# An attention and mixer kernel on one core: last tile of w_theta loaded and decoded earlier, epsilon added on VectorE, one q product moved behind the first theta product

## The chip, the cores and the metric

One core of one Trainium2 chip. The time is device microseconds (us) of one execution of the whole program; of the kernel before there are three timed runs, 1085.14, 1086.68 and 1089.25, and their median, 1086.68, is what the changed kernel's median is compared with. A further execution was taken with the hardware profiler; it took 1086.08 us.

## What is computed

The reference is a chain of three parts over 8 batches of 576 tokens and 512 channels (8 heads of 64). Attention without softmax comes first, then a mixer whose token weights turn with an angle theta, then a second mixer. What the change touches is attention and the start of the first mixer:

```python
kv = np.einsum('bhsd,bhse->bhde', k, v)
out = np.einsum('bhsd,bhde->bhse', q, kv)
rms = np.sqrt(np.mean(out * out, axis=-1, keepdims=True) + 1e-06)
x = out / rms * g_norm                      # then (b, s, h*d)
theta = x @ w_theta
zr, zi = x * np.cos(theta), x * np.sin(theta)
y = np.einsum('ts,bsd->btd', w_tok_r, zr) + np.einsum('ts,bsd->btd', w_tok_i, zi)
u = x + y
x = u + np.maximum(u @ w_ch, 0.0)
```

The inputs q, k, v are 32-bit floats; the weights (w_theta, w_tok, w_ch and so on) come as 64-bit floats and are turned into 32-bit ones on the chip.

## The kernel before

A batch's 576 tokens are worked in five tiles: four of 128 tokens (0 to 3) and one of 64 (4). Most products are made of three 16-bit products (a high and a low half of each operand, helper `mm3`, lines 101 to 107). In batch 0 alone, q products, turns and theta products are 32-bit ones, which take several passes over the array. The work around the change is all in batch 0, at the start of the program, and goes through these steps:

- **Loads.** SP's queue asks for everything in the order in which the program is written: w_theta's four tiles (`theta_weight`, `load` at line 148), k and v of batch 0 (L382, L386, L392), the first 128 tokens of q (L406), the rest of q (`load_q`, L421), then the token weights `wmr` (L233).
- **Decoding** (`decode`, lines 161 to 174) of a 64-bit weight tile: one ScalarE pass (L164) and three VectorE passes (L172, L173, L174) in which 32-bit words are shifted and joined. w_theta goes into `wt`; the token weights into `wm0v`, `wm1v` and so on, and from there into high and low halves `wmh` (L245, ScalarE) and `wml` (L247, VectorE).
- **kv** (L438), the product of k and v, ends in `kvbd`.
- **attend** (lines 450 to 506), written `a0` to `a4` in the schedule: the q product `po` (L458), its square on ScalarE (L471), the sum over a head's 64 channels on VectorE (`ss`, L473), on GpSimd the addition of epsilon (L474) and the power of -0.5 (`ri`, L475), the scaled `x` on VectorE (L478), and in batch 0 a turn of `x` on TensorE (`px`, L488) that ScalarE copies out (`xt`, L490).
- **rotate** (lines 551 to 593), written `r0` to `r4`: the theta product `pt` (L563; for tile 4 it is L604), then in turns ScalarE and VectorE: rounding (L574, L578), sine, absolute value, cosine (L581 to L583), the product of both with `x` (L586), the 16-bit halves `zh` (L590) and `zl` (L593).
- **outer** (`X0` to `X4`): the token mix, 16-bit products `pa` and `pb` of `zh`, `zl` with `wmh`, `wml` (lines 105 to 107).

Each of these is a generator, and one line of text sets the order in which they are started (line 1027); every start also lets all open ones go one step further (`go` and `advance`, lines 985 to 997). `w` in it starts the next token weight. What the engines get in the end is settled by a list scheduler, which moves instructions within each engine's list except those that are held in the written order (`tc.keep_in_program_order`, here by `held` for batch 0, lines 425 to 427). Each engine then works off its list strictly in order.

Of the kernel before, what the change touches and what calls it, by code (L numbers as in the profile page):

```python
# [14 lines left out]
ALU = mybir.AluOpType  # L15
# [13 lines left out]
def attn_mixer_kernel(  # L29
# [4 lines left out]
    nc = tc.nc  # L34
# [3 lines left out]
    KD = DM // P  # L38
# [25 lines left out]
    def bank(name):  # L64
        return ps.tile([P, 512], F32, tag="ps", name=name)
# [58 lines left out]
    eps = const.tile([P, H], F32, name="eps")  # L124
# [9 lines left out]
    wt = const.tile([P, KD, DM], F32, name="wt")  # L134
# [11 lines left out]
    def load(dst, src):  # L146

        tc.keep_in_program_order(nc.sync.dma_start(dst, src))

    wp = []  # L150
# [3 lines left out]
    def gated(ins, behind):  # L154

        tc.add_manual_dep(
            ins.ins, (turned_xt[0] if behind is turned_xt else turned_zh[behind]).name,
            mybir.DependencyInfo(mybir.DependencyClass.NoSync, mybir.DependencyReason.DATA), reason="behind",
        )

    def decode(val, raw, behind=None):

        bits = val.bitcast(I32)
        first = nc.scalar.activation(val, raw[..., 1].bitcast(F32), AF.Copy, scale=2.0**-112)  # L164
        if behind is not None:
            gated(first, behind)
        if wp:

            tc.keep_in_program_order(first)
        yield  # L170
        place = placed if wp else lambda ins: ins
        place(nc.vector.tensor_scalar(bits, bits, 3, None, ALU.logical_shift_left))  # L172
        place(nc.vector.scalar_tensor_tensor(bits, raw[..., 0], 29, bits, ALU.logical_shift_right, ALU.bitwise_or))  # L173
        place(nc.vector.scalar_tensor_tensor(bits, raw[..., 1], -(2**31), bits, ALU.bitwise_and, ALU.bitwise_or))  # L174
# [23 lines left out]
    def theta_weight(j):  # L198

        if w_theta.dtype == F32:  # L200
            load(wt[:, j], w_theta[j * P:(j + 1) * P])
            yield
        else:
            raw = stg.tile([P, S, 2], I32, tag="raw", name=f"wt{j}r")[:, :DM]
            load(raw.rearrange("p n w -> p (n w)"), w_theta.bitcast(I32)[j * P:(j + 1) * P])
            yield
            yield from decode(wt[:, j], raw)

    def theta_split(j):

# [186 lines left out]
    def load_heads(b, whole=True):  # L397
        o = Batch()
        o.b, o.zh = b, None
        o.kv = []  # L400
        for r in range(NR + 1 if b < 2 else 3):
            load_kv(o, r)
        o.q = fp.tile([P, HP, SM + P], F32, tag="q", name=f"q{b}", bufs=1)
        qs = qT[b].rearrange("h p s -> p h s")
        if b == 0:
            nc.sync.dma_start(o.q[:, :, :P], qs[:, :, :P])  # L406
        elif whole:
            load_q(o, 0)
        return o

    def load_q(o, at):
        qs = qT[o.b].rearrange("h p s -> p h s")
        if o.b + 1 < B:

            part = qs[:, :, at:]
            (ps_, _), (hs, _), (ss_, _) = part.ap
            parts = [(o.q[:, :, at:], bass.AP(part.tensor, part.offset, [[ps_, P], [hs, HP], [ss_, SM + P - at]]))]
        else:
            parts = [(o.q[:, :, at:S], qs[:, :, at:]), (o.q[:, :, S:], qs[:, :, SM:])]
        for dst, src in parts:  # L420
            ins = nc.sync.dma_start(dst, src)  # L421
            if o.b in (2, 3):
                tc.keep_in_program_order(ins)

    def held(o, ins):
        if o.b == 0:
            tc.keep_in_program_order(ins)
# [22 lines left out]
    def attend(o, r):  # L450

        b = o.b
        if r == 0:
            o.R = mp.tile([P, KD, S], F32, tag="R", name=f"R{b}", bufs=2)
            o.x, o.xt = {}, {}
        po = bank(f"po{b}{r}")
        for hp in range(HP):
            held(o, nc.tensor.matmul(po[:, hp * P:(hp + 1) * P], o.q[:, hp, r * P:(r + 1) * P], kvbd[:, hp, :], start=True, stop=True))  # L458
        po3 = po.rearrange("p (h d) -> p h d", d=D)
        ss = fp.tile([P, H], F32, tag="ss", name=f"ss{b}{r}", bufs=3)  # L460
        ri = fp.tile([P, H], F32, tag="ri", name=f"ri{b}{r}", bufs=3)
        xs = fp.tile([P, 2, DM], F16, tag="xs", name=f"xs{b}{r}", bufs=2) if b else None
        x = o.x[r] = fp.tile([P, DM], F32, tag="x", name=f"x{b}{r}", bufs=NR + 1)
        xt = o.xt[r] = fp.tile([P, 2, KD, P], F16, tag="xt", name=f"xt{b}{r}", bufs=NR + 1)
        if b == 0:
            xt = o.xt[r] = xt.rearrange("p a k t -> p (a k t)").bitcast(F32).rearrange("p (k t) -> p k t", k=KD)

        x3 = x.rearrange("p (h d) -> p h d", d=D)
        place = beside(o)
        yield  # L470
        place(nc.scalar.activation(x3, po3, AF.Square, scale=D**-0.5))  # L471
        yield
        held(o, place(nc.vector.tensor_reduce(ss, x3, axis=AX.X, op=ALU.add)))  # L473
        nc.gpsimd.tensor_tensor(ss, ss, eps, ALU.add)  # L474
        nc.gpsimd.tensor_tensor(ri, ss, mhalf, ALU.pow)  # L475
        yield
        yield
        held(o, place(nc.vector.tensor_tensor(x3, po3, ri.unsqueeze(2).to_broadcast([P, H, D]), ALU.mult)))  # L478
        n = SR if r == NR else P
        R, by = o.R[:, :, r * P:r * P + n], SW if r == NR else gs  # L480
        if r == NR and b == 2:
            R = x[:, :KD * SR].rearrange("p (k t) -> p k t", k=KD)
        if b == 0:

            yield
            px = bank(f"px{r}").rearrange("p (k t) -> p k t", k=KD)
            for kk in range(KD):
                held(o, nc.tensor.transpose(px[:, kk, :], x[:, kk * P:(kk + 1) * P], ident))  # L488
            yield
            turned_xt.append(nc.scalar.activation(xt, px, AF.Copy, scale=gt).ins)  # L490
            if r == NR:
                nc.scalar.activation(R, px[:, :, :n], AF.Copy, scale=by)
            return
        if b > 1:
            yield
        place(nc.scalar.activation(xs[:, 0, :], x, AF.Copy))
        yield
        place(nc.vector.tensor_tensor(xs[:, 1, :], x, xs[:, 0, :], ALU.subtract))
        place(nc.sync.dma_start_transpose(xt.rearrange("p a k t -> p (a k) t"), xs.rearrange("p a d -> p (a d)")))
        if 0 < b < 3 and r < NR:  # L500
            return
        for _ in range(3 if b > 1 else 2):
            yield
        place(nc.scalar.activation(R, xt[:, 0, :, :n], AF.Copy, scale=by))
        yield
        place(nc.vector.scalar_tensor_tensor(R, xt[:, 1, :, :n], by, R, ALU.mult, ALU.add))
# [13 lines left out]
    def beside(o):  # L520
        return placed if o.b > 1 else lambda ins: ins

    def channel_weights():

        if w_ch.dtype == F32:
            return [weight_tile(stg, w_ch, wc, j, DM, SW, "wc") for j in range(KD)]
        raws = []
        for j in range(KD - 1):
            raw = stg.tile([P, S, 2], I32, tag="raw", name=f"wc{j}r")[:, :DM]
            nc.sync.dma_start(raw.rearrange("p n w -> p (n w)"), w_ch.bitcast(I32)[j * P:(j + 1) * P])  # L530
            raws.append(raw)
        return [weight_tile(stg, w_ch, wc, j, DM, SW, "wc", raw=raw, behind=g) for j, (raw, g) in enumerate(zip(raws + [None], (NR, NR + 1, NR + 1, NR + 2)))]
# [452 lines left out]
    def go(unit, lead=False):  # L985
        advance()
        next(unit)
        (leading if lead else pending).append(unit)
# [16 lines left out]
    def spare(n=1):  # L1005
        for _ in range(min(n, len(extra))):
            go(extra.pop(0))
# [6 lines left out]
    for j in range(KD):  # L1014
        if j == 2:
            o = load_heads(0)
        go(theta_weight(j))
        if j == max(2, 1):
            load_q(o, P)
    for part in range(2):  # L1020
        go(kv(o, part))
# [2 lines left out]
    extra += mix_weights()  # L1024
    nxt = load_heads(1)
    later = channel_weights()
    for what in "a0 . . a1 a4 a2 a3 r0 w r1 r4 w r2 r3 X0 X1 k w w w X4 A0 X2 A1 s0 s1 s2 s3 X3 A4 A2 A3 U".split():
        if what == ".":
            advance()
        elif what == "w":  # L1030
            spare()
        elif what == "k":
            for part in range(2):
                go(kv(nxt, part))
        elif what == "U":
            go(mixed(o))
        else:
            unit = {"a": attend, "r": rotate, "X": outer, "s": residual}[what[0].replace("A", "a")]
            go(unit(nxt if what[0] == "A" else o, int(what[1])))
# [42 lines left out]
    for b in range(B):  # L1082
# [71 lines left out]
        o, nxt = nxt, after  # L1154
# [52 lines left out]
```

## Time and profile before

| | us |
|---|---|
| median of three runs | 1086.68 |
| the profiled execution | 1086.08 |
| its span | 1084.3 |
| TensorE busy (98% of the span) | 1064.3 |
| VectorE busy (74%) | 806.8 |
| ScalarE busy (52%) | 565.0 |
| GpSimd busy (17%) | 186.6 |

The span runs from the first to the last instruction of the profiled execution. Times of rows count from its start. In what follows the engines have the profile's names: PE is TensorE, DVE VectorE, ACT ScalarE, POOL GpSimd, SP the engine that asks for most transfers.

### The profile page before, as it was taken

How to read it: one execution, taken by the hardware profiler on the slowest of the kernel's cores; microseconds unless marked ns; L12 is line 12 of the kernel's file. 1: busy time of each engine (PE TensorE's matmuls, PEld its weight loads, DVE VectorE, ACT ScalarE, POOL GpSimd, SP SyncE). 2: the span in 40 equal slices, each digit the busy share in tenths (PEclk: the TensorE clock that was granted, in tenths of full speed). 3: DMA queues.
4: the chain of work that ended last, by engine and by line, in shares of the span. 5: the costliest groups of instructions: out<-in, count | busy, mean ns of one | idle time of the engine just before them, and what ended most of it. 6: DMA issues, size and time to landing. Idle time of an engine off the chain costs nothing.

```text
span 1084.3 us, 21468 instructions
## 1 busy us (share of the span) xinstructions
PE 1064.3 (98%) x8857; PEld 812.4 (75%) x8857; DVE 806.8 (74%) x1431; ACT 565.0 (52%) x950; POOL 186.6 (17%) x256
## 2 busy tenths in 40 slices
PE   6999998999999999999999999999999999999998
PEld 4677775777668767686777777777777777777776
DVE  4999887887978878888463866858585775858484
ACT  3868456465654655657241735455463645446360
POOL 3140041714526335252000000000000000000000
PEclk9999999999999999999999999999999999999999
DMA  9618469748669387553738111020201101020101
GB/s 359 245 32 241 77 151 266 204 103 224 172 158 243 103 226 195 129 148 74 213 117 280 62 39 50 11 77 12 78 1 46 44 28 61 12 77 7 39 2 44
DMA packets 141367, 126.05 MB, mean 116 GB/s; under 512 B 88213, under 2 KB 117525, under 8 KB 141269
## 3 DMA queue, kind: packets, MB, share of 16 engines
q1 hardware_dynamic: 135888, 104.23, 34.8%
q0 software_dynamic: 5376, 20.45, 5.2%
q8 instruction: 69, 1.13, 0.4%
q14 instruction: 30, 0.24, 0.1%
q10 hardware_dynamic: 4, 0.00, 0.0%
HBM read 74.25 MB, written 29.88 MB: 96 GB/s over the span
## 4 chain that ended last, share of the span: by engine, by line
PE 88%; DVE 5%; DMA 2%; ACT 2%; POOL 1%; issue 1%; SPq 0%; DVEq 0%; POOLq 0%; ACTq 0%
PE py L105 5%; PE py L106 5%; PE py L107 5%; PE pa L105 5%; PE pa L106 5%; PE pa L107 5%; PE na L105 4%; PE na L107 4%; PE na L106 4%; PE po L458 3%; PE pr L105 2%; PE pr L107 2%; PE pr L106 2%; PE nc L107 2%; PE nc L105 2%; PE pc L107 2%
## 5 line engine op out<-in xcount | busy, mean ns | idle before, releaser
L105 PE MATMUL py<-wmh,zh 128*128 128x320 f16 (+1 forms) x468 | 134.2, 287 | 0.3 <-DMA zh<-zt 0.3
L106 PE MATMUL py<-wml,zh 128*128 128x320 f16 (+1 forms) x468 | 134.2, 287 | 0.0
L107 PE MATMUL py<-wmh,zl 128*128 128x320 f16 (+1 forms) x416 | 119.3, 287 | 0.0
L107 PE MATMUL na<-gh,wbl 128*128 128x288 f16 x384 | 109.3, 286 | 0.0
L106 PE MATMUL pa<-o,wah 128*128 128x288 f16 x384 | 109.2, 286 | 0.0
L106 PE MATMUL na<-gl,wbh 128*128 128x288 f16 x384 | 109.1, 286 | 0.0
L105 PE MATMUL pa<-o,wah 128*128 128x288 f16 x384 | 108.3, 286 | 0.0
L107 PE MATMUL pa<-o,wal 128*128 128x288 f16 x384 | 107.8, 286 | 0.0
L105 PE MATMUL na<-gh,wbh 128*128 128x288 f16 x384 | 106.0, 286 | 0.2
L870 DVE TENSOR_TENSOR gl<-sum,gh 128x1152 f16<-128x1152 f32 x48 | 64.9, 1353 | 21.9 <-ACT gh L869 21.9
L106 PEld LDWEIGHTS <-wbh 128*128 128x128 f16 x672 | 65.7, 98 | 17.7 <-issue 0.9
L105 PEld LDWEIGHTS <-wah 128*128 128x128 f16 x672 | 65.8, 98 | 16.6
L106 PEld LDWEIGHTS <-wah 128*128 128x128 f16 x672 | 65.8, 98 | 16.6
L107 PEld LDWEIGHTS <-wal 128*128 128x128 f16 x672 | 65.8, 98 | 16.6
L105 PEld LDWEIGHTS <-wbh 128*128 128x128 f16 x672 | 65.7, 98 | 16.6
L107 PEld LDWEIGHTS <-wbl 128*128 128x128 f16 x672 | 65.7, 98 | 16.6
L106 PE MATMUL pr<-ul,wch 128*128 128x256 f16 (+1 forms) x256 | 73.0, 286 | 0.0
L105 PE MATMUL pr<-uh,wch 128*128 128x256 f16 (+1 forms) x256 | 72.9, 286 | 0.0
L107 PE MATMUL pr<-uh,wcl 128*128 128x256 f16 (+1 forms) x256 | 72.8, 286 | 0.0
L475 POOL TENSOR_TENSOR ri<-ss,mhalf 128x8 f32<-128x8 f32 x40 | 70.9, 1772 | 2.5
L105 PEld LDWEIGHTS <-zh 128*128 128x128 f16 x576 | 56.4, 98 | 17.1 <-ACT zh L590 1.1
L869 ACT ACTIVATE gh<-sum 128x1152 f16<-128x1152 f32 x48 | 55.5, 1156 | 25.5 <-DVE sum L917 25.5
(304 smaller groups left out, 2914.3 us busy)
## 6 DMA issues: line engine op xcount, KB each, us to landing
c<-u2d SPq DMA_DIRECT2D x32, 288.0 KB, 4.4
out<-c SPq DMA_DIRECT2D x64, 144.0 KB, 1.7
q<-in_q SPq DMA_DIRECT2D x6, 1280.0 KB, 6.8
k<-in_k SPq DMA_DIRECT2D x26, 256.0 KB, 5.5
v<-in_v SPq DMA_DIRECT2D x26, 256.0 KB, 5.7
wa_r<-in_w_ch SPq DMA_DIRECT2D x24, 256.0 KB, 4.2
wb_r<-in_w_ch SPq DMA_DIRECT2D x24, 256.0 KB, 4.2
wad<-wa POOLq DMA_DIRECT2D x24, 224.0 KB, 3.8
```

The lines of the kernel that those rows point to most:

```text
L105: nc.tensor.matmul(acc, ah, bh, start=first and i == 0, stop=False, **more)
L106: nc.tensor.matmul(acc, ah, bl, start=False, stop=False, **more)
L107: nc.tensor.matmul(acc, al, bh, start=False, stop=last and i == n - 1, **more)
L458: held(o, nc.tensor.matmul(po[:, hp * P:(hp + 1) * P], o.q[:, hp, r * P:(r + 1) * P], kvbd[:, hp, :], start=True, stop=True))
L475: nc.gpsimd.tensor_tensor(ri, ss, mhalf, ALU.pow)
L869: nc.scalar.activation(h.hi[:, 3:], h.s, AF.Copy)
L870: nc.vector.tensor_tensor(h.lo[:, 3:], h.s, h.hi[:, 3:], ALU.subtract)
```

## The change

It does four things, all of them in batch 0's first steps. The last tile of w_theta is asked for ahead of the rest of q, not behind it. Its three DVE passes are put four steps later in the written order, and held there. Batch 0 adds epsilon on DVE (a new instruction, held in the written order as well), and POOL keeps only the power. In the line of text, `r0` stands ahead of `a3`: the q product of tile 3 is started behind the first theta product.

```diff
-    def decode(val, raw, behind=None):
+    def decode(val, raw, behind=None, ticks=0):
...
         yield
-        place = placed if wp else lambda ins: ins
+        for _ in range(ticks):
+            yield
+        place = placed if wp else tc.keep_in_program_order if ticks else lambda ins: ins
         place(nc.vector.tensor_scalar(bits, bits, 3, None, ALU.logical_shift_left))
...
-            yield from decode(wt[:, j], raw)
+            yield from decode(wt[:, j], raw, ticks=4 if j == KD - 1 else 0)
...
         held(o, place(nc.vector.tensor_reduce(ss, x3, axis=AX.X, op=ALU.add)))
-        nc.gpsimd.tensor_tensor(ss, ss, eps, ALU.add)
+        if b:
+            nc.gpsimd.tensor_tensor(ss, ss, eps, ALU.add)
+        else:
+            held(o, nc.vector.tensor_scalar(ss, ss, 1e-6, None, ALU.add))
         nc.gpsimd.tensor_tensor(ri, ss, mhalf, ALU.pow)
...
         go(theta_weight(j))
-        if j == max(2, 1):
+        if j == KD - 1:
             load_q(o, P)
...
-    for what in "a0 . . a1 a4 a2 a3 r0 w r1 r4 w r2 r3 X0 ...
+    for what in "a0 . . a1 a4 a2 r0 a3 w r1 r4 w r2 r3 X0 ...
```

The scheduler makes new lists of it. On TensorE, in the first steps of batch 0 (names such as `px3` are the step and the tile; the number behind the underscore only tells buffers apart), the kernel before has this, from the turn of tile 0 on:

```order
L488 MATMUL px0_283<-ident_78,x00_257 128x128 x4
L458 MATMUL po02_292<-kvbd_100,q0_145 128x128 x4
L458 MATMUL po03_306<-kvbd_100,q0_145 128x128 x4
L563 MATMUL pt00_320<-wt_102,xt00_258 128x512 x2
L488 MATMUL px1_323<-ident_78,x01_270 128x128 x4
L563 MATMUL pt00_320<-wt_102,xt00_258 128x512 x2
L488 MATMUL px4_336<-ident_78,x04_281 128x128 x4
L563 MATMUL pt01_346<-wt_102,xt01_271 128x512 x4
L488 MATMUL px2_354<-ident_78,x02_299 128x128 x4
L604 MATMUL pt04_369<-xt04_282,wt_102 128x64 x16
L488 MATMUL px3_388<-ident_78,x03_313 128x128 x4
L563 MATMUL pt02_411<-wt_102,xt02_300 128x512 x4
```

and the changed kernel this:

```order
L493 MATMUL px0_283<-ident_78,x00_254 128x128 x4
L460 MATMUL po02_292<-kvbd_100,q0_145 128x128 x4
L568 MATMUL pt00_306<-wt_102,xt00_255 128x512 x4
L460 MATMUL po03_316<-kvbd_100,q0_145 128x128 x4
L493 MATMUL px1_325<-ident_78,x01_270 128x128 x4
L493 MATMUL px4_335<-ident_78,x04_281 128x128 x4
L568 MATMUL pt01_349<-wt_102,xt01_271 128x512 x4
L493 MATMUL px2_357<-ident_78,x02_299 128x128 x4
L609 MATMUL pt04_369<-xt04_282,wt_102 128x64 x16
L493 MATMUL px3_397<-ident_78,x03_323 128x128 x4
L568 MATMUL pt02_411<-wt_102,xt02_300 128x512 x4
```

The q product of tile 3 (`po03`) has moved behind the whole first theta product; the turn of tile 3 (`px3`) still stands ahead of the theta products of tiles 2 and 3.

On VectorE, from the sum of tile 3 (`ss03`) to its scaled `x03`, the kernel before has:

```order
L473 TENSOR_REDUCE ss03_311<-x03_313 128x8
L172 TENSOR_SCALAR wm1v_409<-wm1v_409 128x1152
L174 SCALAR_TENSOR_TENSOR wm0v_344<-wmr0_213,wm0v_344 128x1152
L478 TENSOR_TENSOR x02_299<-po02_292,ri02_298 128x512
L578 SCALAR_TENSOR_TENSOR cs00_334<-cs00_334,pt00_320 128x512
L173 SCALAR_TENSOR_TENSOR wm1v_409<-wmr1_215,wm1v_409 128x1152
L478 TENSOR_TENSOR x03_313<-po03_306,ri03_312 128x512
```

and the changed kernel, from `x02` on:

```order
L483 TENSOR_TENSOR x02_299<-po02_292,ri02_298 128x512
L475 TENSOR_REDUCE ss03_321<-x03_323 128x8
L249 SCALAR_TENSOR_TENSOR wml_104<-wm0v_347,wmh_103 128x2x576
L176 SCALAR_TENSOR_TENSOR wm1v_409<-wmr1_212,wm1v_409 128x1152
L479 TENSOR_SCALAR ss03_321<-ss03_321 128x8
L591 TENSOR_TENSOR cs00_315<-cs00_315,x00_254 128x1024
L583 SCALAR_TENSOR_TENSOR cs01_354<-cs01_354,pt01_349 128x512
L249 SCALAR_TENSOR_TENSOR wml_104<-wm1v_409,wmh_103 128x2x576
L483 TENSOR_TENSOR x03_323<-po03_316,ri03_322 128x512
```

The sum of tile 3 now stands behind `x02`, its epsilon two long passes further on, and `x03` behind three more passes.

And where the changed VectorE list takes up the token weights, from `x01` to that `x02`:

```order
L483 TENSOR_TENSOR x01_270<-po01_263,ri01_269 128x512
L174 TENSOR_SCALAR wm0v_347<-wm0v_347 128x1152
L475 TENSOR_REDUCE ss02_297<-x02_299 128x8
L175 SCALAR_TENSOR_TENSOR wm0v_347<-wmr0_210,wm0v_347 128x1152
L479 TENSOR_SCALAR ss02_297<-ss02_297 128x8
L483 TENSOR_TENSOR x04_281<-po04_274,ri04_280 128x512
L174 TENSOR_SCALAR wm1v_409<-wm1v_409 128x1152
L176 SCALAR_TENSOR_TENSOR wm0v_347<-wmr0_210,wm0v_347 128x1152
L583 SCALAR_TENSOR_TENSOR cs00_315<-cs00_315,pt00_306 128x512
L175 SCALAR_TENSOR_TENSOR wm1v_409<-wmr1_212,wm1v_409 128x1152
L483 TENSOR_TENSOR x02_299<-po02_292,ri02_298 128x512
```

In the kernel before, `x02` stood ahead of the first tile's rounding pass (L578) and of the second pass over `wm1v` (L173); now it stands behind both.

## Rows read from the trace of the kernel before

**Rows 1.** who PE waited for, whole span: us in total, times, longest us

```profile
PE pa L107 <- DVE zh L647: 1.1, 1, 1.1
...
PE pa L105 <- ACT zh L590: 1.0, 1, 1.0
PE px L488 <- DVE x L478: 1.0, 1, 1.0
...
PE po L458 <- DMA q<-in_q: 0.4, 1, 0.4
```

**Rows 2.** stretches: us, PE, PEld, DVE, ACT, POOL busy (count), PEclk, DMA share, GB/s

```profile
40.00:48.00 8.00, 8.00 (x50) 5.29 (x49) 8.00 (x12) 7.45 (x15) 0.00 (x0) 1.00 0.32 127
```

**Rows 3.** order of time, PE: start us, us, engine line op out<-in xcount [idle before it]

```profile
17.35 2.90 PE L458 MATMUL po<-kvbd,q 128*128 128x128 f32 x16 [0.40 <-DMA q<-in_q]
...
21.23 0.66 PE L488 MATMUL px<-ident,x 128*128 128x128 f32 x4 [0.97 <-DVE x L478]
...
21.72 1.95 PE L458 MATMUL po<-kvbd,q 128*128 128x128 f32 x16
...
23.51 1.88 PE L563 MATMUL pt<-wt,xt 128*128 128x512 f32 x4
...
28.40 3.60 PE L563 MATMUL pt<-wt,xt 128*128 128x512 f32 x8
...
32.28 3.68 PE L604 MATMUL pt<-xt,wt 128*128 128x64 f32 x32
...
35.80 0.61 PE L488 MATMUL px<-ident,x 128*128 128x128 f32 x4
...
43.11 0.27 PE L105 MATMUL pa<-wmh,zh 128*128 128x256 f16 x1
...
61.30 1.06 PE L458 MATMUL po<-kvbd,q 128*128 128x128 f32 x8
```

**Rows 4.** order of time, DVE and two ACT rows, 6 to 38 us

```profile
6.01 0.16 DVE L118 COPY gn<-pg 128x1 f32<-128x1 f32 x1 [6.01 <-PE pg L117]
...
17.62 0.69 DVE L473 TENSOR_REDUCE ss<-x 128x8 f32<-128x512 f32 x1 [0.42 <-ACT x L471]
...
18.59 0.67 ACT L164 ACTIVATE wt<-wt3r 128x512 f32<-128x512 f32 x1 [1.01 <-DMA wt3r<-in_w_theta]
...
19.30 0.43 DVE L172 TENSOR_SCALAR wt<-wt 128x512 int32<-128x512 int32 x1 [0.99 <-ACT wt L164]
...
20.48 0.69 DVE L478 TENSOR_TENSOR x<-po,ri 128x512 f32<-128x512 f32 x1
...
21.98 0.69 ACT L490 ACTIVATE xt<-px,gt 128x512 f32<-128x512 f32 x1 [1.09 <-PE px L488]
...
23.87 0.76 DVE L172 TENSOR_SCALAR wm0v<-wm0v 128x1152 int32<-128x1152 int32 x1 [0.91 <-ACT wm0v L164]
...
29.03 1.38 DVE L174 SCALAR_TENSOR_TENSOR wm0v<-wmr,wm0v 128x1152 int32<-128x1152 int32 x1
...
30.93 0.67 DVE L578 SCALAR_TENSOR_TENSOR cs<-cs,pt 128x512 f32<-128x512 f32 x1
...
32.80 0.68 DVE L478 TENSOR_TENSOR x<-po,ri 128x512 f32<-128x512 f32 x1
...
33.40 1.34 DVE L247 SCALAR_TENSOR_TENSOR wml<-wm0v,wmh 128x1152 f16<-128x1152 f32 x1
...
36.53 1.21 DVE L586 TENSOR_TENSOR cs<-cs,x 128x1024 f32<-128x1024 f32 x1
```

**Rows 5.** order of time, POOL, 18 to 32 us

```profile
18.46 0.20 POOL L474 TENSOR_TENSOR ss<-ss,eps 128x8 f32<-128x8 f32 x1 [11.16 <-DVE ss L473]
...
18.74 1.67 POOL L475 TENSOR_TENSOR ri<-ss,mhalf 128x8 f32<-128x8 f32 x1
...
29.28 2.63 POOL L475 TENSOR_TENSOR ri<-ss,mhalf 128x8 f32<-128x8 f32 x1
```

**Rows 6.** a stretch, PE alone: us, PE busy (count), PEclk, DMA share, GB/s

```profile
14.80:17.00 2.20, 2.07 (x8) 1.00 1.06 402
```

More of the change, by code (lines that the diff above doesn't have):

```diff
@@ L1026, in attn_mixer_kernel @@
     later = channel_weights()
-    for what in "a0 . . a1 a4 a2 a3 r0 w r1 r4 w r2 r3 X0 X1 k w w w X4 A0 X2 A1 s0 s1 s2 s3 X3 A4 A2 A3 U".split():
+    for what in "a0 . . a1 a4 a2 r0 a3 w r1 r4 w r2 r3 X0 X1 k w w w X4 A0 X2 A1 s0 s1 s2 s3 X3 A4 A2 A3 U".split():
         if what == ".":
```

## The prediction

> **What bounds the kernel now.** I read first the list of whom TensorE waited for [rows 1], then the table of stretches [rows 2], then the instructions in order of time between 14 and 44 us, engine by engine [rows 3 to 6]. The page's table says that TensorE is busy 1064.3 us of a span of 1084.3, so any change can at best take from the 20.0 us in which it stands, and the larger part of those is the wait for the first data. The waits that the change can reach are in [rows 1]: 0.4 us for the rest of q, 1.0 us for the first scaled `x`, and two later ones, 1.1 us and 1.0 us, that the z work of batch 0 and batch 1 ends. The second reading is that the start is not bound by one engine: from 40 to 48 us PE and DVE are busy 8.00 of 8.00 us and ACT 7.45 [rows 2]. Such a stretch is sensitive to order: every engine works off its list in turn, and an operation that slips behind long passes on DVE is late by the sum of these passes, whoever waits for it. The third reading is when the token mix starts. PE runs its 32-bit products without a gap from the first turn, 21.23, to the first mix product, 43.11 [rows 3].
>
> **The loads.** The rest of q landed just before 17.35, where PE began on it, and the last tile of w_theta just before 18.59, where ACT began on it [rows 3, 4]. That is 1.24 us for the tile. With the order changed the rest of q lands at about 17.35 + 1.3 = 18.65, and the tile about 2.5 us sooner (the rest of q has twice its bytes), near 16.1, ahead of tile 0's square on ACT. The second and third q product thus start 1.3 us later. What hides it is the wait for tile 0's first `x`, 0.97 us ahead of the turn [rows 3]: the 16 passes of 2.90 us would end at 21.55 at the latest, and the first turn goes at 21.15 to 21.55, against 21.23. I take 21.15, since half of these passes then run at the later, faster pace (below), and keep 21.55 for the range.
>
> **Epsilon on DVE.** Five additions leave POOL (0.20 us where nothing holds them [rows 5]) and five small DVE passes come in. The trace has no such pass; the nearest are a copy of 128x1, 0.16 us, and the pass over 128x512, 0.43 us [rows 4]. I take 0.16, as eight elements are nearer to one than to 512. A DVE pass starts 0.08 us ahead of the end of the one before (32.80 + 0.68 against 33.40 [rows 4]), so each adds 0.08 us to the list, 0.4 us in all. For tile 0 the sum ends at 18.31, epsilon at 18.51, the power starts 0.15 us later as the addition did (18.31 to 18.46), takes 1.67 [rows 5], and `x` follows 0.07 us behind: 20.40, against 20.48. The three passes of the tile's decoding, 0.46 + 0.72 + 0.69 us, run from 18.43 to 20.30 in that time and cost nothing; the cover is the power itself.
>
> **Where it is lost: the turn of tile 3.** The first theta product was cut in two by a turn and began at 23.51. Now it can begin when `xt` is copied, 21.98 - 0.08 + 0.69 = 22.6 [rows 4], and it is whole. The price is on DVE. By the list of the changed kernel, `x01` comes when the second power is done: the sum of tile 1 follows `x00` (20.40 + 0.61 = 21.01), its epsilon ends at 21.9, the power at 23.7, so `x01` at 23.75 and the first pass on `wm0v` at 24.35, against 23.87 [rows 4]. From there the list is dense. I count each pass without its last 0.08 us, from [rows 4]: 0.68 for a shift on 1152 columns, 1.26 for the long two-operand passes (1.34), 0.60 for 512 columns, 1.13 for the product with `x` (1.21), 0.08 for epsilon. From 24.35 up to tile 3's epsilon stand two shifts (1.36), five of 0.60 (the sums of tiles 2 and 3, `x04`, `x02` and the first rounding; 3.00), one epsilon (0.08) and five long passes (two on `wm0v`, two on `wm1v`, one `wml`; 6.30), 10.74 together. Epsilon of tile 3 thus starts at 35.1. Behind it stand a product (1.13), a rounding (0.60) and `wml` (1.26) ahead of `x03`; with epsilon 3.07, so `x03` starts at 38.15, and its turn 0.75 us later (20.48 to 21.23), at 38.9. The power of tile 3 is over by 36.9 and is not what holds it.
>
> PE would be ready earlier. From 21.15: a turn 0.49, a q product 0.90 (two take 21.72 to 23.51), theta from 22.65 with 3.44 (eight passes of 3.60 without the last 0.16), q product 0.90, turn 0.49, the turn of tile 4 when its `x` is done (24.35 + 2.62 + 0.75 = 27.7), theta from 28.3 to 31.75, the turn of tile 2 at 24.35 + 7.02 + 0.75 = 32.1, then tile 4's theta, 3.52, to 36.1 [rows 3]. So PE stands from 36.1 to 38.9, 2.8 us, ahead of `px3`, where it had no gap. In the kernel before that turn went at 35.80 [rows 3]. All behind it on PE (two theta products, then the token mix) is the same, so the mix starts 38.9 - 35.8 = 3.1 us later, at 46.2 against 43.11.
>
> **The sum.** Loads 0 (0 to +0.4), epsilon and decoding -0.1 up to the first turn, which is in the 3.1 already, tile 3's turn +3.1. Behind 46 us the list of both kernels is the same work; I let the 3.1 us stand, because the z work of tiles 2 and 3 hangs on the theta products that come late, and batch 1 queues behind it on DVE and ACT. Against the profiled execution, 1086.08 + 3.1 = 1089.2. The median of the runs shown lies 0.6 us above that execution, so I forecast 1086.68 + 3.1 = **1089.8 us**, 0.29% slower. A measurement of this kernel can tell about 0.5%, 5.4 us, from no change; by that the likeliest verdict is no change.
>
> **The rivals.**
>
> *The wait is paid back.* PE stands 2.8 us at `px3`, but the two waits of 1.1 and 1.0 us that follow [rows 1] are ended by DVE and ACT; if these are no later than before, PE arrives late and waits less. For it speaks that the first tile's rounding comes earlier (below). Against it, that the wait for `zh` at line 590 belongs to batch 1, whose work stands behind batch 0's on DVE. 1089.8 - 2.1 = 1087.7.
>
> *The early first tile decides, and it is faster.* The first rounding pass (L578) starts at 24.35 + 5.16 = 29.5, against 30.93 [rows 4]. If sines and z work, not PE, set the start of the mix, all that follows is 1.4 us earlier: 1086.68 - 1.4 = 1085.3. It decides if `x03` is done before PE has finished tile 4's theta, that is if the DVE list up to it is 2.8 us shorter than my sum, two of its long passes.
>
> *PE's pace.* Eight passes of a q product take 2.07 us between 14.8 and 17.0 [rows 6] and 1.06 us at 61.30 [rows 3]: up to some point in the second and third q product PE runs at the pace of its lower level, 1.2 against 2.4 GHz. The granted clock is printed as 1.00 for that stretch too [rows 6], so I go by the pace. Now PE stands 1.7 us, not 0.4, ahead of these products. If the rise comes only behind them, 16 passes take 3.9 us and the first turn goes at 22.5, 1.35 us late; if it comes behind the first theta product as well, 3.44 us more. Of these 4.8 us the gap at `px3` covers 2.8: 2.0 us on top, 1091.8, and more where DVE, fed late, is late itself. The Trainium skill (TensorE: Matmul & The Clock Gate, Part 1) states that the throttled clock is the default, that activity releases it and that an idle stretch brings it back, which speaks against this change; the row above agrees with the first half, and no row here shows a return.
>
> *The power is held by the decoding.* A power that started at 29.28 took 2.63 us, not 1.67, and started under a DVE pass with two operands in memory that ran from 29.03 to 30.41 [rows 4, 5]: it waited for that pass. In the changed order the power of tile 0 starts at 18.66, just where the three decoding passes run until 20.30. If it slips in at the end of the first (18.86), 0.2 us are lost; if all three hold it, it ends at 20.3 + 1.5 = 21.8 and `x00` comes at 21.9, 1.4 us late, and the DVE list with it: 1089.8 + 1.4 = 1091.2. The passes wait for one another's results and leave short gaps, which speaks against. The Trainium skill (GPSIMD Engine Reference, Key points) states that GpSimd shares its memory interfaces with VectorE's two-port and two-input instructions; by this rule the sum would be 1091.2, and the 2.63 us agree with it.
>
> **How the numbers follow.** Chances: forecast 0.50, paid back 0.18, faster 0.10, pace 0.12, held power 0.10. The range runs from a little under the faster case to a little over the pace case, as medians of three move by some tenths of a us (the three runs of before span 4.1): 1084.8 to 1092.6. It leaves out about 0.05 below and 0.08 above. Faster by over 0.5% (under 1081.2) needs more than any case gives: 0.02. Slower by over 0.5% (over 1092.1) is the upper half of the pace case, 0.06, and tails of the held power and the forecast, 0.03: 0.09. The rest, 0.89, is no change.
>
> **What would show it.** In the changed profile: the first turn at 21.1 to 21.6; three decoding passes between tile 0's sum and `x00`; a new wait of PE at the turn (line 493) of 2 to 3 us near 36 to 39 us, ended by DVE's `x` (line 483); the first `pa` product at about 46; and the two later waits of PE at about their size. If there is no such wait at the turn, or it is under 1 us, the count on DVE is wrong. If the wait is there and the time is within 1 us of before, it was paid back. Theta passes of 0.86 us in place of 0.43 would show the pace case, and a first power of over 3 us the held one.

## The result, and the profile after

The changed kernel took 1094.8 us (median of six runs, 1092.67 to 1095.83), the kernel before 1087.05 in six runs: a ratio of 1.0065, 95% interval 1.0049 to 1.0081. It is slower by 7.75 us where +3.1 was forecast, and the time lies above the range. The profiled execution took 1093.35 us, its span is 1091.6.

The list of whom TensorE waited for, changed kernel (us in total, times, longest), against [rows 1]:

```profile
PE px L493 <- DVE x L483: 2.3, 1, 2.3
...
PE pa L105 <- ACT zh L595: 2.0, 1, 2.0
...
PE po L460 <- DMA q<-in_q: 1.8, 1, 1.8
...
PE pa L107 <- DVE zh L652: 0.5, 1, 0.5
```

The wait at tile 3's turn is there, 2.3 us where 2.8 was forecast; the wait for q grew from 0.4 to 1.8; of the two later waits one shrank from 1.1 to 0.5 and the other grew from 1.0 to 2.0. TensorE in order of time, changed kernel (start us, us, engine, line, operation, count, idle before it), against [rows 3]:

```profile
19.41 3.78 PE L460 MATMUL po<-kvbd,q 128*128 128x128 f32 x16 [1.78 <-DMA q<-in_q]
...
22.98 1.06 PE L493 MATMUL px<-ident,x 128*128 128x128 f32 x4
...
40.67 0.63 PE L493 MATMUL px<-ident,x 128*128 128x128 f32 x4 [2.27 <-DVE x L483]
41.13 8.73 PE L568 MATMUL pt<-wt,xt 128*128 128x512 f32 x16
49.70 0.27 PE L105 MATMUL pa<-wmh,zh 128*128 128x256 f16 x1
...
93.07 0.28 PE L105 MATMUL pa<-wmh,zh 128*128 128x256 f16 x1 [2.03 <-ACT zh L595]
```

The token mix of batch 0 starts at 49.70 against 43.11, 6.6 us late, and that of batch 1 at 93.07, 6.7 us late against this row of the kernel before:

```profile
86.37 0.28 PE L105 MATMUL pa<-wmh,zh 128*128 128x256 f16 x1 [0.99 <-ACT zh L590]
```

VectorE, and GpSimd's first power, changed kernel, against [rows 4, 5]:

```profile
19.02 0.17 DVE L479 TENSOR_SCALAR ss<-ss 128x8 f32<-128x8 f32 x1
19.10 0.42 DVE L174 TENSOR_SCALAR wt<-wt 128x512 int32<-128x512 int32 x1
...
20.28 0.69 DVE L176 SCALAR_TENSOR_TENSOR wt<-wt3r,wt 128x512 int32<-128x512 int32 x1
21.09 0.69 DVE L483 TENSOR_TENSOR x<-po,ri 128x512 f32<-128x512 f32 x1
...
26.02 0.76 DVE L174 TENSOR_SCALAR wm0v<-wm0v 128x1152 int32<-128x1152 int32 x1 [0.50 <-ACT wm0v L164]
...
36.76 0.16 DVE L479 TENSOR_SCALAR ss<-ss 128x8 f32<-128x8 f32 x1
...
39.84 0.68 DVE L483 TENSOR_TENSOR x<-po,ri 128x512 f32<-128x512 f32 x1
...
19.34 1.71 POOL L480 TENSOR_TENSOR ri<-ss,mhalf 128x8 f32<-128x8 f32 x1 [11.70 <-DVE ss L479]
```

The list from the first pass on `wm0v` runs as counted: epsilon of tile 3 comes 10.74 us behind it (counted 10.74), `x03` 13.82 (counted 13.80). But it starts at 26.02 and not 24.35. Two stretches of the changed kernel (us; busy time of PE, PEld, DVE, ACT, POOL; PEclk; DMA share; GB/s), the first against [rows 2]:

```profile
40.00:48.00 8.00, 7.33 (x17) 3.39 (x18) 7.20 (x11) 6.48 (x12) 0.00 (x0) 0.79 0.37 149
184.00:192.00 8.00, 5.86 (x42) 2.68 (x37) 2.94 (x4) 3.68 (x6) 0.00 (x0) 0.79 1.03 290
```

The granted clock fell to its lower level right behind the wait at the turn, from 41.4 to 44.8 us: the two theta products behind it took 8.73 us where 16 passes at the upper level take 7.03. It fell again from 188.2 to 191.6, behind a wait for a transfer. The Trainium skill (TensorE: Matmul & The Clock Gate, Part 1) states that an idle stretch brings the throttled clock back; with this the trace agrees here, for waits of 2.27 and 2.14 us. So the first theory, A, was: 2.3 us at the turn, 1.7 for each fall, and a rise to the full clock at 24.3 us in place of 19.2.

### The profile page after: what moved, and what is told of

It is laid out like the page before. It is cut to its first block, busy times and chain, and to the rows that moved or that the text cites. A ratio compares the mean times of both kernels' runs of the same rounds, so it can differ in the third digit from the quotient of the medians.

```text
span 1091.6 us, 21470 instructions
## 1 busy us (share of the span) xinstructions
PE 1068.9 (98%) x8857; PEld 815.4 (75%) x8857; DVE 809.0 (74%) x1436; ACT 567.0 (52%) x950; POOL 182.6 (17%) x251
## 4 chain that ended last, share of the span: by engine, by line
PE 89%; DVE 4%; DMA 3%; ACT 1%; issue 1%; POOL 1%; SPq 0%; DVEq 0%; ACTq 0%; POOLq 0%
PE py L105 5%; PE py L106 5%; PE py L107 5%; PE pa L107 5%; PE pa L105 5%; PE pa L106 5%; PE na L105 4%; PE na L107 4%; PE na L106 4%; PE po L460 3%; PE pr L105 3%; PE pr L107 3%; PE pr L106 3%; PE pt L106 2%; PE pt L107 2%; PE pt L105 2%
```

## Experiments

Medians are compared with those of runs of the kernel before that were made beside them (1086.74 to 1087.46); ratios have 95% intervals.

**e1: line of text put back.**

```diff
-... "a0 . . a1 a4 a2 r0 a3 w ...
+... "a0 . . a1 a4 a2 a3 r0 w ...
```

> The changed kernel with the line of text put back (tile 3's q product ahead of the first theta product); loads, epsilon and decoding stay as changed. Theory A (the list and the clock): by the VectorE list the scaled x of tile 3 stands 9.6 us of passes behind the first pass on wm0v and not 13.2, so TensorE's wait at tile 3's turn (2.27 us in the changed kernel) falls under 0.5 us, and the stretch of half clock right behind it (3.41 us at 0.5 in the changed profile, 1.7 us of work) goes with it: 1094.8 - 2.3 - 1.7 = 1090.8 us, or 1089.1 if the second stretch of half clock at 188 us goes too. The wait for the rest of q (1.78 us) and the late rise of the clock (24.3 against 19.2 us) stay. Rival B (the loads decide all): the late q and the late rise alone make the loss, so the time stays within 1 us of 1094.8.

Measured: 1087.73, ratio 1.0004 (0.9991 to 1.0017), with no wait at tile 3's turn and a first mix product at 44.19. The other three parts together cost nothing that can be measured, and rival B (the loads decide all) falls. But the line gives back 7 us, more than theory A has for it.

**e2: old order of loads.**

```diff
-        if j == KD - 1:
+        if j == max(2, 1):
             load_q(o, P)
```

> The changed kernel with the rest of q asked for ahead of w_theta's last tile again; all else as changed. Theory A: the wait for q falls from 1.78 to about 0.4 us, the clock rises near 19 to 21 us, the first turn goes at 21.2 to 21.6 in place of 22.98; but the last tile of w_theta comes at about 18.6, its three VectorE passes are held ahead of the first x and make that x 1 us late, and the wait at tile 3's turn stays at 2 to 3 us, as that is set by the VectorE list: 1094.8 - 1 to 2 = 1092.8 to 1093.8. Rival B (the loads decide all): back to within 1 us of 1087.05.

Measured: 1092.8, ratio 1.0046 (1.0033 to 1.0059), as theory A has it; B falls again.

**e3: the line of text alone, in the kernel before.**

> The kernel before with the new line of text alone (tile 3's q product behind the first theta product). Theory A: TensorE waits 2 to 3 us at tile 3's turn near 36 to 39 us, the granted clock then falls to 0.5 for some 3.4 us: 1087.05 + 2.5 + 1.7 = 1091.3. Rival C (the list without the clock): the wait is there and no stretch of half clock follows: 1089.6. Rival B (the loads decide all): within 1 us of 1087.05.

Measured: 1090.21, ratio 1.0021 (1.0006 to 1.0037), a wait of 1.6 us at the turn and a stretch of half clock behind it. Alone, the line costs about what was forecast; A and C can't be told apart by it. Its runs lie in two groups, seven from 1086.33 to 1090.25 and five from 1092.28 to 1093.37; the profiled one, 1087.45, is of the lower group. Batch 1's mix starts at 87.95, 1.6 us late.

**e4: work that nobody reads in both waits.**

```diff
+        if b == 0 and r == 1:
+            for _ in range(6):
+                held(o, nc.tensor.matmul(po[:, :P], ident, ident, start=True, stop=True))
...
+            if r == 3:
+                for _ in range(16):
+                    held(o, nc.tensor.transpose(px[:, 0, :], ident, ident))
```

> The changed kernel with work that nobody reads put into TensorE's two new waits: 6 products of the identity with itself ahead of the second q product (about 1.56 us at the pace there, in a wait of 1.78) and 16 turns of the identity ahead of tile 3's turn (about 1.7 us in a wait of 2.27); the real products overwrite them. Nothing that VectorE, ScalarE or the loads do is changed. Theory A (half of the loss is the clock): the rise comes at 19 to 21 us in place of 24.3 and the fall behind tile 3's turn goes: 1094.8 - 1 to 1.5 - 1.7 = 1091.6 to 1092.1, while the first data wait and tile 3's x are as late as before. Rival C (the waits alone): no gain, within 0.5 us of 1094.8.

Measured: 1093.88, ratio 1.0054 (1.0042 to 1.0066), between the two forecasts. The first mix product came at 46.49, 3.2 us sooner than in the changed kernel, and yet under 1 us of it is left in the time: TensorE now stood 3.5 us ahead of batch 1's mix, for `zh`. This sent the search to what lies between the two mixes. Batch 1's q products, kernel before and then changed kernel (TensorE, and the row of SP's queue that groups the five DMA transposes of batch 1's `x`: start of the first, us to the end of the last):

```profile
61.30 1.06 PE L458 MATMUL po<-kvbd,q 128*128 128x128 f32 x8
63.48 2.84 PE L458 MATMUL po<-kvbd,q 128*128 128x128 f32 x24
70.41 1.06 PE L458 MATMUL po<-kvbd,q 128*128 128x128 f32 x8
...
71.62 12.90 SPq L499 DMA_TRANSPOSE xt<-xs  x5
```

```profile
67.32 1.05 PE L460 MATMUL po<-kvbd,q 128*128 128x128 f32 x8
69.14 1.06 PE L460 MATMUL po<-kvbd,q 128*128 128x128 f32 x8
74.28 2.84 PE L460 MATMUL po<-kvbd,q 128*128 128x128 f32 x24
...
73.97 16.25 SPq L504 DMA_TRANSPOSE xt<-xs  x5
```

Eight passes are one tile's product. Before, four tiles stood ahead of the last 36 mix products of batch 0 and one behind; now two stand ahead and three behind. The third `x` of batch 1 is late by that, its transposes spread from 12.9 to 16.25 us, and `zh`, for which batch 1's mix waits, hangs on them. That is theory D: the change has turned a list (the order of steps in it; tile 3's turn is another thing) 30 us behind the place that it edits. (In e4 the filling had turned it back, but put one VectorE pass on the transposes' operands late: 17.59 us for the five.)

**e5: batch 1's q products ahead of the mix again.**

```diff
-... X4 A0 X2 A1 s0 s1 s2 s3 X3 A4 A2 A3 U
+... X4 A0 X2 A1 A4 A2 s0 s1 s2 s3 X3 A3 U
```

> The changed kernel with one edit far behind the change: in the line of text A4 and A2 (two q products of batch 1) are started ahead of s0 and X3, so that three of batch 1's q products stand ahead of the last 36 token-mix products of batch 0 again, as in the kernel before; in the changed kernel the list has only two of the five ahead of them and three behind. The first 60 us are unchanged. Theory D (the change turned the list of batch 1): the five DMA transposes of batch 1's x take 12.4 to 13 us from first to last in place of 16.25, TensorE's wait for batch 1's zh (2.0 us) falls to 1 us or less, and the time falls by about 3 us: 1094.8 - 3 = 1091.8. Theory A (the turn of tile 3 and the clock make all of the loss): nothing behind 60 us matters, 1094.3 or more.

Measured: 1090.8, ratio 1.0034 (1.0021 to 1.0046). Four q products, not three as the expectation has it, stand ahead of the mix products, as in the kernel before. The same rows of this kernel, and the start of batch 1's mix:

```profile
66.79 1.05 PE L460 MATMUL po<-kvbd,q 128*128 128x128 f32 x8
68.61 2.84 PE L460 MATMUL po<-kvbd,q 128*128 128x128 f32 x24
75.54 1.06 PE L460 MATMUL po<-kvbd,q 128*128 128x128 f32 x8
...
90.34 0.27 PE L105 MATMUL pa<-wmh,zh 128*128 128x256 f16 x1
...
74.52 12.38 SPq L504 DMA_TRANSPOSE xt<-xs  x5
```

The transposes are back to 12.38 us, the wait for `zh` at the start of batch 1's mix is gone, and that mix starts at 90.34. VectorE's and ScalarE's lists turn back with TensorE's. Four of the 7.75 us lay here.

**e6: epsilon back on GpSimd**, all else as changed.

> The changed kernel with epsilon back on GpSimd in batch 0; loads, decoding and line of text as changed. Its list has three q products of batch 1 ahead of the last 36 token-mix products again, and tile 3's turn still behind the long VectorE passes. Theory D: the wait of 2 to 3 us at tile 3's turn stays, the transposes of batch 1 take about 13 us, 1094.8 - 3 = 1091.8. Theory A: epsilon costs its five passes of 0.08 us in the list and no more: 1094.4.

Measured: 1090.93, ratio 1.0035 (1.0023 to 1.0047), with the old list for batch 1 and the transposes in 13.49 us. So it takes the swap and epsilon on VectorE together to turn that list: with either of them back (e1, e6), and with the swap alone (e3), it stays.

**e7: both places mended.** Besides the edit of e5:

```diff
-... r0 a3 w r1 r4 w r2 r3 X0 ...
+... r0 a3 w r1 r4 r2 w r3 X0 ...
```

> The changed kernel with both suspected places mended in the line of text: the theta product of tile 2 is started ahead of tile 3's turn (r2 one place forward), which fills TensorE's wait of 2.27 us, and A4 and A2 ahead of X3 as in the run before the last. Loads, epsilon and decoding stay as changed. Theory A and D together: no wait over 0.5 us at tile 3's turn, the first mix product at 45 to 46.5 us in place of 49.7, batch 1's transposes in about 13 us: 1087.5 to 1089.5, level with the kernel before. If loads or epsilon cost something that does not go through these two places, it stays above 1090.5.

Measured: 1087.14, ratio 1.0003 (0.9990 to 1.0016): the whole loss is gone, with loads, epsilon, decoding and the swap still in. TensorE in this kernel at the place of the wait:

```profile
38.27 3.65 PE L568 MATMUL pt<-wt,xt 128*128 128x512 f32 x8
41.76 0.60 PE L493 MATMUL px<-ident,x 128*128 128x128 f32 x4
43.46 3.70 PE L568 MATMUL pt<-wt,xt 128*128 128x512 f32 x8 [1.10 <-ACT xt L495]
47.00 0.27 PE L105 MATMUL pa<-wmh,zh 128*128 128x256 f16 x1
```

Tile 2's theta product fills the wait; what is left is 1.10 us for the copy of tile 3. The mix still starts at 47.00, 3.9 us later than in the kernel before, and that costs nothing in the end. Tile 2's theta product ahead of the turn without the edit of e5 was not run.

**e8: e5 with the wait for q filled** (the first piece of e4's edit).

> The kernel with batch 1's q products ahead of the mix (first of this call) and, on top, 6 products of the identity with itself on TensorE in its wait for the rest of q; nobody reads them. Theory A: with no standing there the clock rises at 12 to 20 us in place of 24.3, the second and third q product take 2.0 to 2.9 us in place of 3.78, the first pass on wm0v comes about 1 us sooner and so does tile 3's x: 1 us less than the kernel without the filling, in the median 0.5 to 1.7. If the pace there is paid for by nothing later, no difference (within 0.4).

Measured: 1090.59, 0.2 us under e5, though the clock in its profile stood at the upper level from 13.8 to 37.6 us (in that of e5 at the lower one from 16.9 to 23.7). But then it was at the lower level from 37.6 to 44.5 us, twice as long as in e5 (40.8 to 44.2):

```profile
38.00:44.00 6.00, 4.54 (x9) 2.51 (x10) 5.30 (x7) 5.24 (x10) 0.34 (x1) 0.50 0.91 359
...
39.46 1.09 PE L496 MATMUL px<-ident,x 128*128 128x128 f32 x4 [2.71 <-DVE x L486]
40.34 9.09 PE L571 MATMUL pt<-wt,xt 128*128 128x512 f32 x16
49.27 0.27 PE L105 MATMUL pa<-wmh,zh 128*128 128x256 f16 x1
```

Tile 3's `x` came 0.7 us sooner than in e5 and the mix at the same time (49.27 against 49.22). What was won ahead of the turn was lost at it, so this run does not show what the late rise costs by itself.

**e10: e5 with the wait at the turn filled** (the second piece).

> The kernel with batch 1's q products ahead of the mix (1090.8 us) and, on top, 16 turns of the identity on TensorE ahead of tile 3's turn, where it waits 2.2 us; the real turn overwrites them, and tile 3's x comes no sooner. Theory A (clock): no stretch of half clock follows the turn, the two theta products behind it take 6.9 to 7.1 us in place of 8.7, the mix starts 1.7 us sooner: 1089.1. If what counts there is the late x alone: 1090.4 to 1091.2.

Measured: 1090.59, ratio 1.0035 (1.0024 to 1.0046), the same as e5. What was to be filled was filled:

```profile
37.53 1.92 PE L494 MATMUL px<-ident 128*128 128x128 f32 x16
39.86 0.66 PE L496 MATMUL px<-ident,x 128*128 128x128 f32 x4 [0.41 <-DVE x L483]
40.35 7.03 PE L571 MATMUL pt<-wt,xt 128*128 128x512 f32 x16
47.22 0.27 PE L105 MATMUL pa<-wmh,zh 128*128 128x256 f16 x1
...
88.41 0.28 PE L105 MATMUL pa<-wmh,zh 128*128 128x256 f16 x1 [0.49 <-ACT zh L598]
...
72.04 14.75 SPq L507 DMA_TRANSPOSE xt<-xs  x5
```

The theta products took 7.03 us, the fall is gone (PEclk 1.00 from 40 to 48 us), the mix starts 2.0 us sooner than in e5 and batch 1's 1.9 us sooner, and the time is the same. But the filling changed more than the clock, as in e4: VectorE's list behind 46 us is another, and the transposes take 14.75 us and not 12.38. So filling gains nothing in either place (e8, e10), but what a fall costs by itself is not shown, and theory A is not ended.

The granted clock of the runs speaks for a part of theory A. Averaged over a kernel's runs it is 0.9960 in e5, 0.9962 in e3, 0.9976 in e10 and 0.9982 in e7; in the kernel before it is 0.9979 to 0.9984. Of the 3.7 us between e5 and e7 the clock would make 2.4 (an estimate: 0.0022 of 1090 us), if TensorE's pace counted everywhere.

**e9: the turned list alone**, forced on the kernel before by a dependence.

> The kernel before, with one dependence added and nothing else: two of batch 1's q products (tiles 4 and 2) must follow the last token-mix product of batch 0's tile 3, so that two of the five stand ahead of the last 36 mix products and three behind, as in the list of the changed kernel. All up to 60 us is as before. Theory D: the five DMA transposes of batch 1's x take 15 to 16.5 us from first to last in place of 12.9, TensorE's wait for batch 1's zh grows by 2 us or more, 1087.4 + 3 to 4 = 1090.4 to 1091.4. Rival (the turned list costs only where TensorE is late already): within 1 us of 1087.4.

Measured: 1090.56, ratio 1.0032 (1.0022 to 1.0042), +3.55 us. The front is as before (first mix product at 43.5); then:

```profile
61.69 1.06 PE L469 MATMUL po<-kvbd,q 128*128 128x128 f32 x8
63.87 1.06 PE L469 MATMUL po<-kvbd,q 128*128 128x128 f32 x8
69.83 2.84 PE L469 MATMUL po<-kvbd,q 128*128 128x128 f32 x24
...
89.05 0.28 PE L105 MATMUL pa<-wmh,zh 128*128 128x256 f16 x1 [2.46 <-ACT zh L601]
...
70.23 16.19 SPq L510 DMA_TRANSPOSE xt<-xs  x5
```

Theory D holds without any other part of the change, though the wait for `zh` grew by 1.5 us and not by 2. The lateness adds up: batch 1's mix starts 2.68 us late here and 3.97 us late in e5, 6.65 together, and 6.70 late in the changed kernel.

**e11, e12: old loads in e5 and in e7.**

> The kernel with batch 1's q products ahead of the mix (1090.8 us), with the rest of q asked for ahead of w_theta's last tile again. By the prediction's term for the loads (0 to 0.4 us): 1090.4 to 1090.8. By the difference that undoing the loads made in the changed kernel (1094.8 to 1092.8, where batch 1's list was turned in both): 1088.8.

> The kernel with tile 2's theta product ahead of tile 3's turn and batch 1's q products ahead of the mix (1087.14 us), with the rest of q asked for ahead of w_theta's last tile again. If the new loads cost what they cost in the changed kernel, 1087.1 - 2.0 = 1085.1, faster than the kernel before by 0.2%; if they cost 0 to 0.4 us, as the prediction had it, 1086.7 to 1087.1, level with it.

Measured: 1093.84 (ratio 1.0059, 1.0040 to 1.0078) and 1091.88 (1.0046, 1.0028 to 1.0064). Neither expectation was right: the old order of loads makes both kernels slower. VectorE in e12:

```profile
18.50 0.17 DVE L479 TENSOR_SCALAR ss<-ss 128x8 f32<-128x8 f32 x1
19.77 0.43 DVE L174 TENSOR_SCALAR wt<-wt 128x512 int32<-128x512 int32 x1 [1.09 <-ACT wt L164]
...
21.68 0.69 DVE L483 TENSOR_TENSOR x<-po,ri 128x512 f32<-128x512 f32 x1
```

VectorE stands 1.09 us for a tile that lands late, and tile 0's `x` is held behind its three passes. Is it the loads, or the holding?

e11 is e2 with the edit of e5, and that gains nothing here: 1093.84 against 1092.8, with overlapping intervals. In the profiles the transposes do fall from 15.25 to 12.36 us, and batch 1's mix follows that of batch 0 by 42.5 us and not 47.0; but e11's first mix starts 4.1 us later (50.99 against 46.90), as q came at 18.93 and not 17.20 with the same order of loads. Whether that is so in every execution is not shown.

**e13, e14: the same two kernels, the passes neither held nor put four steps later** (`ticks=0`).

> The kernel with batch 1's q products ahead of the mix, with the old order of loads as in the run that took 1093.84 us, and the last w_theta tile's three VectorE passes no longer held ahead of tile 0's x (that is how the kernel before has them: one of the three stands behind x). If the 3.0 us that the old loads cost there (1090.8 to 1093.84) came from the held passes, which then wait for a tile that lands late, tile 0's x comes at 20.5 in place of 22.8 us and the time is 1090.4 to 1091.2. If the loads themselves are worth it, 1093 or more.

> The kernel with both places mended (1087.14 us), with the old order of loads, which made it 1091.88, and the three passes no longer held ahead of tile 0's x. Held passes to blame: back to 1086.7 to 1087.5. Loads to blame: 1091 or more.

Measured: 1091.78 (ratio 1.0036, 1.0022 to 1.0050) and 1087.2 (0.9997, 0.9985 to 1.0009). For e14 that settles it: with the old loads, the holding with its four steps was to blame, by itself or by the lists that followed from it. e13 fell between its two forecasts; its ratio is that of e5, but the interval reaches that of e11. Its runs lie apart by the granted clock: three with a mean of 0.998 took 1088.11 to 1089.84 us, seven with 0.995 took 1091.38 to 1093.45.

**e15: the new loads alone, in the kernel before.**

> The kernel before with the new order of loads alone (w_theta's last tile ahead of the rest of q). By the prediction's term, 0 to 0.4 us: 1087.0 to 1087.8, with TensorE's wait for q at 1.7 us in place of 0.4 and the first turn within 0.4 us of 21.2. If the loads are worth what the old order cost in the two runs with held decoding, 1083 to 1084; if they cost 2.0 us as between the changed kernel and the one with old loads, 1089.

Measured: 1087.88, ratio 1.0010 (0.9997 to 1.0022). They gain nothing and may cost 1 us; the first turn came at 22.71.

**e16: the line alone, mended in both places, in the kernel before.**

> The kernel before with the line of text alone: tile 3's q product behind the first theta product, tile 2's theta product ahead of tile 3's turn, and batch 1's q products ahead of the mix; loads, epsilon and decoding as before. If the swap's whole cost lies in these two places: level with the kernel before, 1086.5 to 1087.5, and faster than it only if the earlier first tile brings something: under 1086.

Measured: 1087.31, ratio 1.0004 (0.9992 to 1.0016). Mended, the swap costs nothing and brings nothing. No kernel here beats the one before.

## Why the prediction was wrong

- **Tile 3's turn, +3.1: right in place, near in size, and the size is in part luck.** The list on VectorE was counted to 0.02 us, and the wait came where it was said. With only this place left of the loss (e5) the kernel is 1.0034 times as long, 3.4 us in the medians; the line alone costs 2.75 (e3). But the mix was to start 3.1 us late and the rest to follow it. In e5 it starts 6.1 us late, as the late q and the fall behind the turn, which the forecast had not, come on top of the wait, and batch 1's mix starts 4.0 us late; in e7 the mix starts 3.9 us late and nothing is lost. So the start of the first mix does not by itself set the end.
- **What is known of that place:** what mends it is shown, tile 2's theta product ahead of the turn, together with the edit of e5 (e7, e16). How the place costs its 3.4 us, by the late `x`, the clock or the lists behind, stays open. e7 is 3.4 us below e10, though their batch 1 mixes start at 88.10 and 88.41. In the two profiles, 4.6 us apart, 1.7 us are a fall of the clock from 183.6 to 187.0, which e7's has not, and 1.9 us are longer waits for transfers (at 103, 184 and 326 us); whether they come with the kernel or with the execution is not shown.
- **The step that failed: "Behind 46 us the list of both kernels is the same work; I let the 3.1 us stand."** The work is the same, its order is not. The scheduler put two more of batch 1's q products behind the last 36 mix products; that it did so because batch 0's times changed in its model is likely, not shown. Undoing that in the changed kernel gives 4.0 us back (e5), doing it alone to the kernel before costs 3.55 (e9). The prediction compared the lists up to tile 3's `x` and no further. With what is left in e5, 0.34%, the 0.32% of e9 make 0.66%; the change costs 0.65%. With the old order of loads the same edit gained nothing (e2, e11).
- **Loads, 0 to +0.4: the place was off, the price near.** The first turn was to go by 21.55 and went at 22.98, as q came at 19.41 and not 18.65 and the 16 passes behind it took 3.78 us at the lower level; the list on VectorE started late by it. In e15, which has nothing but the new loads, the first turn went at 22.71. In the end the loads alone cost 1.1 us with an interval that takes in 0 (e15). **Epsilon and decoding, -0.1:** as passes they cost what was said (0.17 us each, pitch 0.08), and with the swap back the three together cost nothing (e1); but epsilon is one of the two edits that it takes to turn the list, which no count of passes shows. That the held decoding costs 4.7 us with the old loads (e12, e14) and nothing that can be measured with the new ones (e7) was not seen either.
- **Paid back:** in the changed kernel the wait for `zh` at line 595 grew from 1.0 to 2.0 us, because the list was turned: in e5 it is gone, and there batch 1's mix makes up 2.1 of the 6.1 us. **Faster:** the first rounding came at 31.17 and not 29.5; in e3 it came at 29.7, and that kernel is slower too. **Pace:** the late rise and a return were both there, and this was the first theory after the result. Its price was not isolated: filling the waits gained 0.2 us at most (e8, e10) but moved the fall or another list, and the kernels with the wait at the turn unfilled (e3, e5) have a granted clock lower by about 0.002. **Held power:** the first power ran 1.71 us from 19.34, under the decoding passes from 19.10 to 20.97: not held. The Trainium skill (GPSIMD Engine Reference, Key points) has GpSimd share its memory interfaces with VectorE passes that read two inputs from memory; the trace agrees for the power at 37.07 (2.48 us, under a product from 36.84), not for this one.

## What to carry to other kernels

Where a scheduler makes the lists, a small edit at one place can turn the order of two steps far behind it: compare the lists of the whole stretch in which the next batch overlaps this one, not only the place of the edit, and follow the longest chain there (here q product, sum, power, `x`, DMA transpose, theta, sine, `zh`). A wait or a slow stretch of the busiest engine need not be worth its length in the end; fill it before it is put into a sum, and look whether the filling has changed other lists too (here it did, e4 and e10). An edit that holds an operation in a place is safe only with the loads it was made for.

## What the runs showed of the hardware

Of the 23 runs of the kernel before that were made beside e1 to e4, eight have a mean granted clock of 1.000 and took 1083.74 to 1087.12 us; the other 15 (0.995 to 0.998) took 1086.79 to 1090.1. The fall at 188 us in the changed kernel followed a wait of 2.14 us for a transfer; the kernel before waits 2.84 us there, and in its profile the clock did not fall. The length of a wait alone does not tell whether the clock falls behind it, and a part of the spread of one kernel's runs goes with the clock.
